# Attention and SwiGLU on one core: the q and k loads of five pairs spread over all partitions, heads paired h and h+4, dummy matmuls in early gaps

## The chip, the cores and the metric

The kernel runs on one core of one Trainium2 chip. The time is device microseconds of that core, from the start of the program to its end. Three runs of the kernel before took 261.69, 265.27 and 265.81 us; the median is 265.27. The profile below is of one further execution, which took 262.36 us.

## The reference

Two steps follow each other. The first is attention for 4 batches, 8 heads, 768 positions and head size 64. Heads 0, 2 and 6 are retrieval heads with the full causal mask; the other five are streaming heads, which keep the first 4 positions (sinks) and a window of 64.

```python
scores = scale * np.matmul(q, k.transpose(0, 1, 3, 2))
causal = rel >= 0
stream_keep = causal & (is_sink | in_win)      # is_sink: pos < 4; in_win: 0 <= rel < 64
mask = np.where(retrieval_head, causal, stream_keep)
a = softmax(np.where(mask, scores, -1e9))
x = np.matmul(a, v)                            # heads side by side: 3072 tokens x 512
```

The second is a SwiGLU block on the 3072 tokens, with weights 512 x 1536, 512 x 1536 and 1536 x 512.

```python
g = x @ w_gate
silu = g * (1.0 / (1.0 + np.exp(-g)))
return (silu * (x @ w_val) @ w_out).astype(np.float32)
```

q, k, v and the weights come in float32; the kernel's matmuls work in float16.

## The kernel before

**Pairs and tiles.** Positions are worked on in tiles of 128. Two tiles of one batch form a pair: 12 pairs, in the order of `QP` (L150), which alternates batches 0 and 1 first. A pair needs three loads of 512 KB: q, k and V (`load`, L332). A load lands in one of 14 `raw` buffers in float32, and is cast to float16 by ACT, DVE or POOL (`cast` for q and k, `castv` for V).

**Turning q and k.** Scores need head dimension on the partitions. For the first five pairs (`n < XPE`, XPE = 5) PE does it: `transposes` makes eight 128x128 transposes of the cast buffer into PSUM, and `evac` copies each half of the pair from there into `qT` or `kT`, with a strided read. For the later pairs a DMA transpose does it (`dmat`). After either, two heads lie one above the other: one on partitions 0 to 63, the other on 64 to 127. Which two is said by `PAIRS`, now (0,2), (4,6), (1,3), (5,7) (L165).

**How the first five pairs are loaded.** There are two DMAs for each of q and k, one for each four heads. Each writes 64 partitions: a partition gets, for each of four heads, four neighbouring rows of 64 floats, so runs of 1 KB. V is always loaded in one DMA over 128 partitions in runs of 512 B; gate and value weights over 128 partitions in runs of 1 KB; output weights over 128 partitions in runs of 2 KB.

**Scores to x.** `plan` (L473) lists for each tile units of up to eight 128x128 score blocks. `scores` multiplies them into two PSUM banks; in the first four tiles (LEAD = 4) masks are added there by PE through `marks`. `exps` takes the exponential on ACT. Later tiles multiply by 0/1 masks m0, m1, m2 on DVE or POOL (`mask`, L553); `mask_fills` makes these masks on DVE early on. `sinks_k` and `sinks_v` copy the sink positions into the blocks of the streaming heads. `values` multiplies with V, which has a column of ones for the sums; `norm` divides; x is turned again by PE (first eight tiles) or DMA.

**The feed-forward block** takes groups of four tiles: `gate` (L725, for gate and value products), tanh on ACT, two products on DVE (L735, L742), `outproj` (L760), a copy out and a store.

**What sets the order.** It is written out. `ORDER` is a list of task numbers, two characters each; tasks are emitted in that order, so it fixes the order on every engine's queue, the DMA issues on SP's included. `WAYS` picks the engine of a task that has a choice, `SLOTS` the buffer or PSUM bank. An engine works strictly through its own order, and a task waits for its inputs and for the earlier users of its buffer. SP issues k0, q0, q1, k1, q2, V0, k2, V1 first, then weights of the first group mixed with V2, k3, q3, k4, V3, q4 (the number is the pair).

**Warming products.** The task `warm` is the first on PE: ten matmuls of the identity with itself (L314), whose result nobody reads.

Of the kernel before, what the change touches and what calls it, by code (L numbers as in the profile page):

```python
# [16 lines left out]
    "070004011K1L061I1J09031T1Q1R1S1o1p1w1x1U1V1y1W1X1f1g0A1q1r1z021d1k1e0C2K202223212B2C2Q2R2S292G2A"  # L17
    "081O1N1P1M1h1Y1Z1a1i1j0D2L2T0B1t1s1u2425261b1c1v2D2E2F2U2W2V2X2Z2a27282c2d1m1n2I2J052Y2b2h2l2m2n"
    "2r2s2o2w0h138r8s8t9192938w8x8y0n14948z90958p8u0E2O2P2N2M8m8n8o8q8v1l0g0z8c8d8e8h8i8j0y8S8T8U8X8Y"
    "0m118k8f8g8Z8l108a8V8W8b2p2q0i169697989B9C9D2e2f2i2g0G31393A3B0l1F9a9b9c9f9g2t2u2v2x0F30360o179E"  # L20
    "9F9h37383F3G3I3J0r1G9d9i9e9j3C3P3D3E3K3L0k1C9V9Q9W9X9R9S3b3c3T3H999A3U3V0J3j3r3s3t0H3234333M3N35"
    "3O3W3X3Y3Z3a0q1D9Y9Z0I3i3o9T9U3p3q3u3x3v3w3y3z0j199G9H9I9L9M9N2j3R3S2k2y2z3Q3d3e3f0p1A9O9J9P0Q55"
    "54523g3h45484E4F0x4041A9AAABAdAeAfA7ATAUACADAV0PAgAh494A2H530u0t15AOAP0w1E18AQARASAnAoAp0MA4A551"
    "580s9KA6A812AJAKAL0v1B0O1HAMAN0K3m3k3l3n0L4MAEAWAXAH0RAFAGAI0S5U590V669k9l9m9n4SAYAZAaAi4T0N4Q4R"
    "4P4N4U4V50579oAsAtAu56AvAw0Z5b4B4J4C4D42434644470cAjAk9p9q9r9s9t4G4H4K4I4LAlAmAxAyAz4Z4a4b4W4X4Y"
    "4e4f9u9v9w9x4j4p4q4u4v4c4d5T5a5Z0U4r9zA0A1A2A34m4s4O4g4t4h4n4i4k4l4oAqArAbAc0T5X5W5H5I5J5A5B5C5K"
    "B2B0B10d7o6E9y4w4x6o6l7E6n4y4z5L7G5M656C6BB3B4B5B7B8B9BABBBCBDBEBFBGBt5Q5d5j5k5e5f5g5h5iBvBwBx5Y"
    "C3BqBrBsBu0Y0bCACBCCBgBhBiBMBN0W686967ByBzBOC0C15N5O5R5P5cCDCEC2C40a7C6DBPBQBlBmBnC5C6C7BWBX5V5D"
    "5E5F5G5SBjBkBYBUBZBa6k6s6r5o5u5r5v5s5wBoBp0XC8C95l5m5p5n5q626L6M5x7I5yBbBcBdBeBf5t5z60636164BRBS"
    "BTBV7D7L7KCFCGCH7HBHBIBJBKBLCICJ6I6J6K6F6G6H6S6N6OCoCpCqCKCLCMCN0fDXDYDZCjCkClD8D9DaDbDADBDC6j6p"  # L30
    "6q7374756t6u70797JDNDODPDG0e7p7wCyCz6P71726Q6R6U6TCrCsD0D1D26Y6Z6a6d6eDQDRDDDEDFDH6v6V6W6X7SD6D3"
    "D4D5D7CeCfCgCPCQCRCSCT6m767T777A787B6w6x7r6yChCiCtCuCv6b6c7u7v7P7Q7R7MCOCwCxCmCnDSDTDU6A6f6g6h6i"
    "7N7OCUCVCWCXCZCaCYCbCc7F7U7V7WDVDW7X7g7h7a7b7c7t7d7e7f6zE4ELEJEMEOE1E2EGENEPEfEgE3E5EiEhEHEIEKEk"
    "ElEmDIDJDKEBECDLDMEDB6EpEqEjErCdDcDdDeDfDh7Y7i7j7m7kEnEo7l84857y7z81828B8380DiDjDkDmDnDo86877x8E"
    "8H8I8FDrDsDtDu7q7Z7n8K8M888N898A8C8D8LEd8GEVEWEXEQEREEEFESEYEZEsEt7s8O8J8P8QDwDxDyDzE6E7E8E9EAEa"
    "EbEcEeETEU8RFJFKFsFEFLFtFWG2FuFTFUFFDvDpFiDqDlE0FVFXFjFkFHFlFnFoFqDgFmFpFrEuFGFIFMFNGAG3G4G7G8G9"
    "GBFYFZFaFxFyFbFcFzG0G1FRG5G6FOFPFvFwFQFSFgEvEwExEyEzF0FdFeFfFhGCF1F2F4F5F6F9FAFBFCF3FDF7F8GDGEGF"
    "GGGHGIGJGKGLGMGNGOGRGPGSGTGQGWGUGVGXGY"
# [3 lines left out]
    "000000000000220020220220011011000000000000000100220222011000000000000001201000000000002001222221"  # L42
    "001001000001000000001010000000000000002201000010010000000000020000000000000020202222000000000000"
    "000001100010000000000012012200000000000001001000020220220000000100000000100001001000002200222020"
    "000000000000000001000000000000000200200000000100000010000000101110210000001000000001200000000000"
    "021020200200000010000000000020000001000000000000000000000000000000000000000000000000000000000000"
    "000000000000000000000000000000000000000001000010000000000000000000000000000000000000000000000000"
    "000000000000000100001100000000010000000000000000000000000000000000000000000000000000000000000001"
    "100001000000001000000000000000000000000000000000000000000000000000000000000000010000110001000010"
    "000000000000000000000000000000000000000000000000000000000000000000000000000000010000000000000000"  # L50
    "0000000000000000000000000000000000000000000000001000100001000001010"
)
SLOTS = (
    "010523746A20796974080CAB6C17BD2493518B8DA51C93B8452163D10106040102241611232063220254440040006220"
    "616201436425612211161624043604454120646214300622320400616445611440622523226261404460004562163226"
    "112612440602263216203446045226106560612261304342246160122543246012162406140236445612242206143605"
    "0023111440102212311231000040220111550227010245020E1113A11049001182013501026303102104125F1004B212"
    "4I3021G3111D1000H0001M4112C1020K2010L2120J1121N0110024000104502081005A11046310472024E51010001511"
    "1243311152025211109021000124000M1011K1000G1120J4105I5120H0121F4001D002280020C4000L2122B100112025"
    "1149401142003241221502260123N5022541137510030103A111100004E521122000114M3002D2003C5012G4000H2110"  # L60
    "L1015J2011K5121B2101I301080101F310012011"
# [57 lines left out]
def kernel(  # L119
# [45 lines left out]
    PAIRS = [(0, 2), (4, 6), (1, 3), (5, 7)]  # L165
# [115 lines left out]
    def mask_fills(x):  # L281
        def run():
            for dst, src in FILLS[x]:
# [3 lines left out]
    FILLS = [[(m0[:, 0:3], BAND0), (m0[:, 3:4], DIAG), (m0[:, 4:6], BAND0), (m0[:, 6:8], DIAG),  # L287
              (m2[:, 2:5], DIAG), (m2[:, 1:2], OWN), (m1[:, 0:2], OWN)],
             [(m2[:, 0:1], FAR), (m1[:, 2:4], FAR)]]

    kT = [const.tile([128, NT, 2, 2, 128], FH, name=f"kT{n}") for n in range(2)]
    QB = 3
# [14 lines left out]
    warm_ps = []  # L307

    def warm(n=10):

        if not warm_ps:
            warm_ps.append(buf("o", [128, 512], FP, "warm"))
        for _ in range(n):
            nc.tensor.matmul(warm_ps[0], ident, ident.unsqueeze(1).to_broadcast([128, 4, 128]),  # L314
                             start=True, stop=True)
# [3 lines left out]
    T_fill1 = P.add("fill1", ["POOL"], fill1)  # L319
    T_warm = P.add("warm", ["PE"], warm, takes=["o"])  # L320
# [11 lines left out]
    def load(kind, n):  # L332
        r = buf("raw", [128, 1024], FP, "raw")
        landed[kind, n] = r
        if kind in "qkx":
            b, pi = QP[n]
            sl = slice(pi * 256, (pi + 1) * 256)
            if kind != "x" and n < XPE:
                for s_ in range(2):
                    nc.sync.dma_start(  # L340
                        out=r[64 * s_:64 * s_ + 64, :].rearrange("p (f x) -> p f x", f=4),
                        in_={"q": q, "k": k}[kind][b, 4 * s_:4 * s_ + 4, sl, :].rearrange(
                            "f (p j) d -> p f (j d)", j=4))
                return
            nc.sync.dma_start(
                out=r.rearrange("p (h x) -> p h x", h=H),
                in_={"q": q, "k": k, "x": v}[kind][b, :, sl, :].rearrange(
                    "h (p j) d -> p h (j d)", j=2))
        elif kind == "o":
            nc.sync.dma_start(  # L350
                out=r.rearrange("p (a n) -> p a n", a=2), in_=wod[:, 2 * n:2 * n + 2, :])
        else:
            nc.sync.dma_start(
                out=r.rearrange("p (a n) -> p a n", a=4),
                in_=(wgd if kind == "g" else wvd)[:, :, n * 256:(n + 1) * 256])
# [46 lines left out]
    def cast(n, kd, x):  # L402
# [4 lines left out]
        if n < XPE:  # L407
# [6 lines left out]
        ks = slice(0, 2) if x is None else slice(x, x + 1)  # L414
        recast(T_c[n, kd, x],
               hqs[n, kd][:, ks].rearrange("p k a (s d) -> p k s a d", s=2),
               landed[kd, n].rearrange("p (k s r j d) -> p k s (r j) d", r=2, s=2, j=2, d=64)[:, ks])
# [24 lines left out]
    def transposes(n, kd):  # L442

        tr = trs[n, kd] = buf("gv", [128, 8, 128], FH, "tr")
        for x in range(8):
            r, j = x // 4, x % 4
            to = x if kd == "q" else 4 * r + 2 * (j % 2) + j // 2
            nc.tensor.transpose(tr[:, to], hqs[n, kd][:, r, j], ident)

    def evac(n, kd, m):  # L450

        dst = turned(n, kd)[:, m].rearrange("c k r x -> c (k r x)")
        if kd == "q":
            copy(T_ev[n, kd][m],
                 dst.rearrange("c (k r p j) -> c k r p j", k=2, r=2, j=4),
                 trs[n, kd].rearrange("c (r j) (k m p) -> c m k r p j", r=2, k=2, m=2)[:, m])
            return
        copy(T_ev[n, kd][m],
             dst.rearrange("c (k l p i) -> c k l p i", k=2, l=4, i=2),
             trs[n, kd].rearrange("c (l i) (k m p) -> c m k l p i", i=2, k=2, m=2)[:, m])  # L460

    def sinks_k(b, m):
# [3 lines left out]
        for cs, k, r in ((slice(0, 128), slice(0, 2), 1), (slice(0, 64), slice(1, 2), 0)):  # L466
# [8 lines left out]
    def plan(t):  # L475

        b, i = TILES[t]
        if i == 0:
# [4 lines left out]
              ([(0, 0, 0, 0), (0, 1, 5, i), (1, 0, 1, -1), (1, 1, 4, i),  # L483
                (1, 0, 2, i), (1, 1, 6, 0), (0, 0, 3, i), (0, 1, 7, 0)], 8, m2)]
        kts = list(range(1, i))
        for ks in (kts[:2], kts[2:]):
            unit = []
            for x, kt in enumerate(ks):
                unit += [(0, 0, 4 - len(ks) + x, kt), (0, 1, 4 + 2 * x, kt),
                         (1, 1, 5 + 2 * x, kt)]  # L490
            if unit:
                us.append((unit, 4 + 2 * len(ks), None))
        return us

    def marks(t, u):
# [3 lines left out]
        if TILES[t][1] == 0:  # L499
            return [(0, BAND0, 3), (3, DIAG, 1), (4, BAND0, 2), (6, DIAG, 2)]  # L500
        if u == 0:
            return [(0, OWN, 2), (2, FAR, 2), (4, OWN, 2), (6, FAR, 2)]
        return [(1, FAR, 1), (2, OWN, 1), (3, DIAG, 1), (4, DIAG, 2)]

    def block(t, p, kt):
# [3 lines left out]
        return kT[b % 2][:, kt, p % 2, p // 2]  # L509
# [8 lines left out]
    def scores(t, u, unit):  # L518
# [4 lines left out]
        for p, s_, c, kt in unit[0]:  # L523
            rows = slice(s_ * 64, s_ * 64 + 64)
            terms.append((c, 1, block(t, p, kt)[rows],
                          qT[t // 2 % QB][rows, half, p % 2, p // 2].unsqueeze(1)))
# [20 lines left out]
    def mask(task, t, u, m):  # L547
        at = 1 if m is m2 else 0
# [286 lines left out]
    for number in P.order():  # L835
# [3 lines left out]
        else:  # L839
            warm(number - P.FILL)  # L840
# [35 lines left out]
```

## Time and profile before

| what | us |
|---|---|
| median of three runs | 265.27 |
| lowest and highest | 261.69, 265.81 |
| the profiled execution's own time | 262.36 |
| its span, first to last instruction | 260.5 |
| PE busy | 243.2 (93%) |
| VectorE (DVE) busy | 165.9 (64%) |
| ScalarE (ACT) busy | 139.2 (53%) |
| GpSimd (POOL) busy | 84.1 (32%) |
| bytes read from HBM | 28.31 MB |
| granted TensorE clock, mean | 0.993 |

A row of digits in the page cuts the span into 40 slices of 6.5 us; a digit is the busy share in tenths, 9 for 90% and more. PE is TensorE's matmuls, PEld its weight loads, SP the engine that issues most DMAs. PEclk is the clock that TensorE was granted. In the chain of waits a line says when a piece began, how long it was, and what it was; the chain goes back from the last instruction through whatever released each step. In a timeline the bracket at the end is the idle time before an instruction, with what ended it.

The PE clock row needs care in the first 18 us. It shows full clock there, but the ten warming products start 0.43 us apart, and later products of the same 512 columns 0.22 us apart.

### The profile page before, as it was taken

The page shows a single profiled execution, that of the slowest core. Times are in us where ns is not written, and L with a number is a line of the kernel's source. Part 1 is how long each engine was busy: PE and PEld are TensorE (multiplying, and loading weights), DVE is VectorE, ACT ScalarE, POOL GpSimd, SP SyncE. Part 2 cuts the span into 40 slices and gives each one's busy share as a digit, 9 for nine tenths or more (in the row PEclk, how much of TensorE's full clock was granted, in tenths as well). Part 3 has the DMA queues.
Part 4 walks back from the last instruction along what each step waited for, and adds up shares of the span by engine and source line. Part 5 has one row for each costly group of instructions (what it writes and reads, how often), then busy time and mean ns, then how long its engine had stood idle before and what let it go on. Part 6 is the DMA issues. An engine that isn't in the chain of part 4 may idle for free.

```text
span 260.5 us, 5165 instructions
## 1 busy us (share of the span) xinstructions
PE 243.2 (93%) x1998; PEld 127.9 (49%) x1998; DVE 165.9 (64%) x294; ACT 139.2 (53%) x219; POOL 84.1 (32%) x114
## 2 busy tenths in 40 slices
PE   6597987969999899989999999999999999999995
PEld 2365764446444445534464454555454554444443
DVE  2338897768497974609989678646773477883211
ACT  1568874738677476647585476644526713421120
POOL 7057945675432354183051018240014200000000
PEclk9999999979999999999999999999999999999999
DMA  6999999999699989999258841344010021101133
GB/s 152 230 236 325 285 219 264 226 273 332 155 327 276 236 168 220 300 254 255 45 77 177 193 102 20 83 116 128 1 23 20 20 64 52 69 3 40 40 126 115
DMA packets 68007, 40.69 MB, mean 156 GB/s; under 512 B 25360, under 2 KB 63504, under 8 KB 67984
## 3 DMA queue, kind: packets, MB, share of 16 engines
q1 hardware_dynamic: 66832, 38.35, 63.5%
q10 hardware_dynamic: 1152, 2.03, 2.1%
q8 instruction: 15, 0.25, 0.4%
q14 instruction: 8, 0.07, 0.1%
HBM read 28.31 MB, written 6.29 MB: 133 GB/s over the span
## 4 chain that ended last, share of the span: by engine, by line
PE 73%; DMA 13%; DVE 6%; SPq 3%; issue 2%; POOL 1%; ACT 1%; DVEq 0%; ACTq 0%
PE banks L725 40%; PE banks L760 22%; DMA raw<-in_v_dram 8%; PE banks L533 5%; PE banks L563 5%; SPq L340 3%; DMA kT<-hq 2%; DMA raw<-in_q_dram 2%; DVE e L553 2%; DVE sil L735 1%; DVE h L742 1%; POOL vt L206 1%; DVE xb L571 1%; PE banks L587 0%; POOL hq L206 0%
## 5 line engine op out<-in xcount | busy, mean ns | idle before, releaser
L545 ACT ACTIVATE e<-banks 128x1024 f16<-128x1024 f32 (+2 forms) x68 | 58.4, 908 | 31.0 <-PE banks L533 22.4
L725 PE MATMUL banks<-xt,wv_sb 128*128 128x512 f16 (+1 forms) x304 | 71.2, 371 | 2.8 <-POOL wv_sb L206 1.5
L725 PE MATMUL banks<-xt,wg_sb 128*128 128x512 f16 (+1 forms) x304 | 69.3, 368 | 1.6 <-POOL wg_sb L206 1.5
L731 ACT ACTIVATE sig<-banks 128x512 f32<-128x512 f32 (+1 forms) x76 | 43.1, 575 | 43.7 <-PE banks L725 38.5
L760 PE MATMUL banks<-wo_sb,h 128*128 128x512 f16 (+2 forms) x300 | 64.8, 371 | 0.0
L735 DVE SCALAR_TENSOR_TENSOR sil<-sig,banks 128x512 f32<-128x512 f32 (+1 forms) x76 | 49.3, 657 | 19.3 <-ACT sig L731 17.4
L742 DVE SCALAR_TENSOR_TENSOR h<-sil,banks 128x512 f16<-128x512 f32 (+1 forms) x76 | 49.0, 656 | 7.8 <-PE banks L725 5.0
L725 PEld LDWEIGHTS <-wg_sb 128*128 128x128 f16 x304 | 28.8, 97 | 33.1 <-POOL wg_sb L206 1.8
L725 PEld LDWEIGHTS <-wv_sb 128*128 128x128 f16 x304 | 28.3, 98 | 32.5 <-issue 2.8
L760 PEld LDWEIGHTS <-h 128*128 128x128 f16 x300 | 28.3, 98 | 32.4 <-issue 0.3
L553 POOL TENSOR_TENSOR e<-e,m 128x1024 f16<-128x1024 f16 (+1 forms) x12 | 22.6, 1883 | 32.4 <-ACT e L545 26.1
L553 DVE TENSOR_TENSOR e<-e,m 128x640 f16<-128x640 f16 (+1 forms) x26 | 20.3, 786 | 16.8 <-ACT e L545 16.6
L206 DVE COPY o_sb<-banks 128x512 f32<-128x512 f32 (+1 forms) x13 | 8.6, 660 | 25.0 <-PE banks L760 23.0
L206 POOL CAST vt<-raw 64x512 f16<-64x512 f32 x27 | 18.2, 675 | 17.7 <-DMA raw<-in_v_dram 14.3
L206 POOL CAST hq<-raw 128x1024 f16<-128x1024 f32 (+1 forms) x16 | 15.8, 989 | 24.7 <-DMA raw<-in_q_dram 11.9
L563 PE MATMUL banks<-vt,e 128*128 128x65 f16 x472 | 18.6, 195 | 4.0 <-POOL vt L206 3.1
L533 PE MATMUL banks<-qT,kT 64*128 64x128 f16 x472 | 21.0, 223 | 0.6 <-ACT e L545 0.4
L563 PEld LDWEIGHTS <-e 128*128 128x128 f16 x472 | 17.4, 98 | 8.4 <-issue 4.6
L204 ACT COPY o_sb<-banks 128x512 f32<-128x512 f32 (+1 forms) x12 | 6.9, 577 | 26.9 <-PE banks L760 23.1
L533 PEld LDWEIGHTS <-kT 64*128 64x128 f16 x472 | 15.1, 96 | 11.4 <-issue 10.0
L571 DVE TENSOR_TENSOR xb<-banks,rc 128x512 f16<-128x512 f32 x24 | 16.6, 691 | 0.8
L206 POOL COPY vt<-vt 2x330 f16<-2x330 f16 x12 | 5.8, 481 | 27.4 <-PE banks L563 27.1
(41 smaller groups left out, 117.2 us busy)
## 6 DMA issues: line engine op xcount, KB each, us to landing
raw<-in_v_dram SPq DMA_DIRECT2D x12, 512.0 KB, 7.5
out_dram<-o_sb SPq DMA_DIRECT2D x16, 256.0 KB, 2.3
raw<-in_k_dram SPq DMA_DIRECT2D x7, 512.0 KB, 5.9
raw<-in_q_dram SPq DMA_DIRECT2D x7, 512.0 KB, 5.8
raw<-in_moe_w_gate_dram SPq DMA_DIRECT2D x6, 512.0 KB, 9.8
raw<-in_moe_w_val_dram SPq DMA_DIRECT2D x6, 512.0 KB, 11.5
raw<-in_moe_w_out_dram SPq DMA_DIRECT2D x6, 512.0 KB, 8.0
raw<-in_k_dram SPq DMA_DIRECT2D x10, 256.0 KB, 9.0
```

What stands on the lines that cost most here:

```text
L206: ENG[task.way].tensor_copy(out=dst, in_=src)
L340: nc.sync.dma_start(out=r[64 * s_:64 * s_ + 64, :].rearrange("p (f x) -> p f x", f=4), in_={"q": q, "k": k}[kind][b, 4 * s_:4 * s_ + 4, sl ...
L533: nc.tensor.matmul(sc[:, c:c + n, :], weights, moving, start=first, stop=last)
L545: nc.scalar.activation(out=to, in_=src, func=AF.Exp, scale=scale)
L553: ENG[task().way].tensor_tensor(out=ev, in0=ev, in1=mm, op=ALU.mult)
L563: nc.tensor.matmul(avs[t][:, odd, n * 66:n * 66 + 65], ee, vv, start=(m == 0), stop=(m == len(bl) - 1))
L571: nc.vector.tensor_tensor(out=xb.rearrange("p n o d -> p o n d"), in0=av[:, :, :, 0:64], in1=rc.to_broadcast([128, 2, 4, 64]), op=ALU.mult)
L725: nc.tensor.matmul(ps, wsb[:, kk, j * 128:(j + 1) * 128], xt[:, kk, c[0]:c[1]], start=(kk == 0), stop=(kk == 3))
L731: nc.scalar.activation(out=sg[g, j, c], in_=gs[g, j, c], func=AF.Tanh, scale=0.5)
L735: nc.vector.scalar_tensor_tensor(out=sl[g, j, c], in0=sg.pop((g, j, c)), scalar=1.0, op0=ALU.add, in1=gs.pop((g, j, c)), op1=ALU.mult)
L742: nc.vector.scalar_tensor_tensor(out=hs[g, j][:, c[0]:c[1]], in0=sl.pop((g, j, c)), scalar=0.5, op0=ALU.mult, in1=vs.pop((g, j, c)), op1=A ...
L760: nc.tensor.matmul(o_open[g, tt, x], hs[g, j][:, tt * 128:(tt + 1) * 128], wo_sb[:, j, lo:hi], start=(j == 0), stop=(j == NJ - 1))
```

## The change

**Loads of the first five pairs.** Each of the two DMAs now writes all 128 partitions: for four heads, a partition gets eight neighbouring rows of one head, a run of 2 KB, in one half of the buffer's columns. Bytes, number of DMAs and their order on SP stay.

**Heads paired h and h+4.** With that layout a cast puts heads h and h+4 one above the other, so `PAIRS` becomes (2,6), (0,4), (1,5), (3,7). Blocks in `plan`, columns of the masks, `marks`, `sinks_k`, `block` and the cast of the later pairs follow from it. The number and sizes of score blocks, exponentials and masks stay. `evac` reads the transposes with other strides, in the same two copies of 512 columns.

**Warming products.** `warm` takes a count and a PSUM bank. PE's order gets 7 ahead of the transposes of k0, 3 ahead of those of q0 and 5 ahead of those of q1.

**The order.** ORDER, WAYS and SLOTS are written anew. Decoded, PE's order is otherwise the same but for a dozen neighbours that change places, and SP's is the same up to its 45th issue. The tasks that change engines: the cast of k1's first half POOL to ACT; the sink copy of tile 1 ACT to POOL, ahead of V's first casts; two V casts (pairs 9 and 11) ACT to POOL; one mask DVE to POOL; two output copies ACT to DVE; two stores SP to ACT.

```diff
 ORDER = (
...
 WAYS = (
...
 SLOTS = (
...
-    PAIRS = [(0, 2), (4, 6), (1, 3), (5, 7)]
+    PAIRS = [(2, 6), (0, 4), (1, 5), (3, 7)]
...
-    FILLS = [[(m0[:, 0:3], BAND0), (m0[:, 3:4], DIAG), (m0[:, 4:6], BAND0), (m0[:, 6:8], DIAG),
-              (m2[:, 2:5], DIAG), (m2[:, 1:2], OWN), (m1[:, 0:2], OWN)],
-             [(m2[:, 0:1], FAR), (m1[:, 2:4], FAR)]]
+    FILLS = [[(m0[:, 0:2], BAND0), (m0[:, 2:4], DIAG), (m0[:, 4:7], BAND0), (m0[:, 7:8], DIAG),
+              (m2[:, 0:3], DIAG), (m2[:, 3:4], OWN), (m1[:, 0:2], OWN)],
+             [(m2[:, 4:5], FAR), (m1[:, 2:4], FAR)]]
...
-    def warm(n=10):
-
-        if not warm_ps:
-            warm_ps.append(buf("o", [128, 512], FP, "warm"))
-        for _ in range(n):
-            nc.tensor.matmul(warm_ps[0], ident, ident.unsqueeze(1).to_broadcast([128, 4, 128]),
+    def warm(n=10, at=None):
+        if at is None:
+            to = buf("o", [128, 512], FP, "warm")
+        else:
+            to = banks[:, at * 512:at * 512 + 512]
+        for x in range(n):
+            nc.tensor.matmul(to, ident, ident.unsqueeze(1).to_broadcast([128, 4, 128]),
                              start=True, stop=True)
...
             if kind != "x" and n < XPE:
                 for s_ in range(2):
                     nc.sync.dma_start(
-                        out=r[64 * s_:64 * s_ + 64, :].rearrange("p (f x) -> p f x", f=4),
+                        out=r[:, 512 * s_:512 * s_ + 512],
                         in_={"q": q, "k": k}[kind][b, 4 * s_:4 * s_ + 4, sl, :].rearrange(
-                            "f (p j) d -> p f (j d)", j=4))
+                            "f (p j) d -> p f (j d)", j=8))
...
     def transposes(n, kd):
 
         tr = trs[n, kd] = buf("gv", [128, 8, 128], FH, "tr")
-        for x in range(8):
-            r, j = x // 4, x % 4
-            to = x if kd == "q" else 4 * r + 2 * (j % 2) + j // 2
-            nc.tensor.transpose(tr[:, to], hqs[n, kd][:, r, j], ident)
+        for j in range(8):
+            nc.tensor.transpose(tr[:, j], hqs[n, kd][:, j // 4, j % 4], ident)
...
         if kd == "q":
-            copy(T_ev[n, kd][m],
-                 dst.rearrange("c (k r p j) -> c k r p j", k=2, r=2, j=4),
-                 trs[n, kd].rearrange("c (r j) (k m p) -> c m k r p j", r=2, k=2, m=2)[:, m])
+            copy(T_ev[n, kd][m], dst.rearrange("c (f n j) -> c f n j", f=4, j=8),
+                 trs[n, kd].rearrange("c j (m n f) -> c m f n j", m=2, f=4)[:, m])
             return
...
-        return kT[b % 2][:, kt, p % 2, p // 2]
+        return kT[b % 2][:, kt, PAIRS[p][0] // 2, PAIRS[p][0] % 2]
...
         else:
-            warm(number - P.FILL)
+            warm((number - P.FILL) % 16, (number - P.FILL) // 16)
```

## The prediction

> **What bounds the kernel now.** First the page's rows of the span in 40 slices (6.5 us each), then the table by stage: time, then busy us and instructions of PE, PEld, DVE, ACT and POOL, then granted clock, DMA share, GB/s.
>
> ```profile
> PE   6597987969999899989999999999999999999995
> PEclk9999999979999999999999999999999999999999
> DMA  6999999999699989999258841344010021101133
> 0.00:18.00 18.00, 12.88 (x86) 6.94 (x88) 5.90 (x14) 7.24 (x12) 7.99 (x26) 1.00 0.97 203
> 18.00:39.00 21.00, 18.20 (x252) 14.10 (x252) 17.11 (x42) 17.40 (x32) 14.58 (x21) 1.00 1.13 273
> 39.00:57.00 18.00, 13.60 (x150) 7.96 (x151) 12.84 (x23) 9.20 (x14) 11.03 (x12) 0.93 1.13 248
> 57.00:258.00 201.00, 198.56 (x1516) 98.88 (x1514) 130.06 (x216) 105.34 (x164) 50.53 (x57) 1.00 0.55 132
> ```
>
> From 57 us to the end PE is busy 198.56 of 201 us: that part is a fixed sum of matmuls, and the DMA engines idle half of it. Before 57 us PE is busy only 44.7 of 57 us while the DMA engines are full in every slice. So the first 57 us are bound by loads, and what they gain is handed to the end nearly whole.
>
> Next, the same table for PE alone, over stretches chosen by what is in flight (last column GB/s):
>
> ```profile
> 3.00:13.50 10.50, 6.74 (x35) 1.00 1.12 236
> 21.00:30.00 9.00, 8.02 (x136) 1.00 1.12 330
> 30.00:39.00 9.00, 7.63 (x77) 1.00 1.13 216
> 42.00:54.00 12.00, 8.37 (x84) 1.00 1.15 217
> 57.00:66.00 9.00, 9.00 (x110) 0.95 1.05 333
> 54.00:55.50 1.50, 1.29 (x27) 0.66 1.11 252
> 55.50:57.00 1.50, 1.50 (x17) 0.50 1.13 320
> 57.00:58.50 1.50, 1.50 (x13) 0.70 1.14 317
> ```
>
> In 3 to 13.5 us only q and k of pairs 0 to 2 move: 236 GB/s. In 21 to 30 us gate and value weights and one V load: 330, at the same DMA share. Where k3 and q3, then k4 and q4 are mixed in: 216 and 217. Last, the chain of waits (start, us) and PE's timeline:
>
> ```profile
> 12.45 9.37 DMA raw<-in_v_dram
> 39.64 12.19 DMA raw<-in_v_dram
> 54.21 1.34 PE banks L563 x25
> 1.36 4.45 PE L314 MATMUL banks<-ident 128*128 128x512 f16 x10 [1.36 <-POOL ident L226]
> 39.56 1.90 PE L725 MATMUL banks<-xt,wg_sb 128*128 128x512 f16 x8 [1.47 <-POOL wg_sb L206]
> 45.67 1.90 PE L725 MATMUL banks<-xt,wv_sb 128*128 128x512 f16 x8 [1.01 <-POOL wv_sb L206]
> 54.21 1.34 PE L563 MATMUL banks<-vt,e 128*128 128x65 f16 x25 [2.32 <-POOL vt L206]
> ```
>
> The chain goes through V of pair 1 (landing at 21.8) and V of pair 3 (51.8, 12 us after its issue: it queues behind other loads). PE waits there for casts that wait for DMA.
>
> **Loads.** The ten q and k loads keep their places in SP's order. Only their shape changes: 2 DMAs of 64 partitions x 4 runs of 1 KB become 2 of 128 partitions x one run of 2 KB. The Trainium skill's "DMA: Bandwidth & Descriptors", in its opening table, puts the line rate at runs of 512 B and more; by it 1 KB runs have nothing to gain and the time stays at 262 to 265. The rows speak otherwise: weight loads in 1 KB runs over 128 partitions and V in 512 B runs make the 330, so run length is not what makes 236. What is left is the half of the partitions; "SBUF — State Buffer", "Door 1: The DMA port swizzle", says that partitions 0..63 reach only 8 of 16 ports, about 218 GB/s. I follow the rows and take 330 GB/s for the new loads (bounds: 236, nothing gained, and the 376 of the best 1.5 us, where the weights for the output run in 2 KB runs).
>
> Worked out: by 54 us the stage rates sum to 13.0 MB. Ten loads of 0.524 MB are 5.24 MB of it; the other 7.76 MB at 330 take 23.5 us, the first bytes come at about 2.6 us, so q and k had 27.9 us (188 GB/s). At 330 they need 15.9: DMA is 12.0 us ahead by then. Of that, the first five (2.62 MB) go from 11.1 to 7.9 us, so V of pair 0 lands 3.2 us sooner. The last five go from 16.8 to 7.9, 1.8 each: V of pair 1 (one more in front) 5.0 sooner, V of pair 3 (four more) some 10.
>
> **Start, to the first value products (20.64 us).** They wait for V of pair 0, then four POOL casts (2.60 us). 3.2 to 4.4 us is to be had. Three things could hold it.
> - The 15 warming products stand ahead of the first three transposes. At the spacing of the old ten (0.43 us) they cost 6.4 us, at 0.22 (12 products in 2.75 us later on) 3.2. The gaps that they fill are 1.80, 0.65 and 1.32 = 3.77 us now and will shrink with the loads, so this cover goes. Ten plus seven in a row keep PE busy from 1.4 us on; I expect full speed from about 7 us, so 3 of them cold, 12 warm, 3.9 us. Then the third transposes start near 10.7 (now 11.73). The work from there to 20.4 that ran at half speed until 16 (128x128 transposes at 1.03 us for eight, 0.62 later) saves 2 to 3 us. PE is ready at about 17, as V is. Bounds: +2.6 us if all stay cold against today's gaps, -3.6 (half of 7.2 us of cold rows).
> - Cast of k1's first half goes from POOL to ACT, ahead of the first exponential: 0.61 us into a hole of 1.62. Behind it stand all exponentials, but k1 lands before the scores are done. Nothing.
> - The sink copy of tile 1 goes from ACT to POOL, ahead of V's first casts: it waits for tile 1's scores, and the four casts and val1 wait behind it. 0.4 us of copies, 0 to 0.6 of waiting; ACT loses a wait of 1.01. I take 0.4.
>
> Sum: 3.5 us sooner (bounds 1.0 and 4.6).
>
> **18 to 39 us** move along: DVE has 17.1 of 21 us of work, so nothing more is gained.
>
> **39 to 57 us.** Here PE waits 1.47, 0.50 and 1.01 us for weight casts and 2.32 for V of pair 3, all behind loads that now come 5 to 10 us sooner. The floors are DVE 12.84 and PE 13.60 less its cold share. That share: 0.34 x 1.29 + 0.5 x 1.5 = 1.2 us, and 0.45 after 57. "TensorE: Matmul & The Clock Gate", "What's actually happening", has the clock fall after an idle window of some 3.4 us; by it a gap of 2.3 us costs nothing, and the gain would be the waits alone. The row shows 0.66 and 0.50 right after that gap, so I count 1.6 us for its going. POOL is next in line: after the mask product (1.41) it casts k4 and V (1.5 and 2.28) in order, 5 us after the exponential, while PE has some 6 us of other work. So the stretch takes about 14 us instead of 18, and 0.4 is saved after it: 4.4 (bounds 2.5, where POOL's order keeps half of the waits, and 5.6, at DVE's floor).
>
> **Everything else.** Evacuations, masks, scores, mask fills and sink copies keep their counts and sizes (two evacuations of 512 columns per transposed half, masks of 1024 and 640): only strides and columns differ. An evacuation costs 0.59 to 0.69 us now with a strided read of PSUM too; at 10% either way 20 of them are 1 us on DVE and ACT, mostly covered. I take 0. Later moves: one V cast of pair 9 to POOL (its POOL hole of 104 to 109 covers 0.6), one mask to POOL (+0.6), two output copies ACT to DVE, two stores from SP to ACT's queue (0.4 of issue each): all where PE has work queued; 0, without that cover 0.7 us each. Stage four has 2.4 us of PE waits: 1 us either way.
>
> **Sum.** 3.5 + 4.4 = 7.9 us off the profiled execution's 262.36 (span 260.5 and 1.9 around it): 254.5. The median shown, 265.27, lies 2.9 above that run, the fastest 261.69. I put half of that on top: **256.0**.
>
> **Rivals.**
> 1. *Taken back by order* (0.15): the warming products stay cold and POOL's order keeps half of the waits: gains 1.0 and 2.5, 258.9, with the same half 260.3. For it: POOL's fixed order, and DVE at 17 of 21 us. Against: POOL has 7 of 18 us free.
> 2. *The loads are no faster* (0.08): 236 comes from something else that q and k have, say head stride. The dummies then fill today's gaps and run 0.1 to 2.6 us over, the clock gives that back: 264 to 266. Against: V has the same head stride and moved in the 330.
> 3. *Slower* (0.06): neighbouring partitions now come from four heads, 196 KB apart, and that access lowers the rate. Break-even is 188 GB/s; at 150 the ten loads take 34.9 us instead of 27.9, all of it on the chain to V of pair 3: 272. Against: V's eight-head loads. It decides if the first stretch shows under 190.
>
> **Numbers.** The forecast has 0.68 (252 to 260), 0.03 lies below. The range takes in the best bounds (10.2 off: 252.2) and rival 1 with the whole offset (258.9 + 2.9 = 261.8). 2% is 5.3 us, about what a measurement of this kernel can tell from no change: under 260.0 is faster. Faster 0.72 (forecast nearly whole, some of rival 1), same 0.20, slower 0.08.
>
> **What would show it.** 300 GB/s or more in 3 to 10 us; V of pair 0 cast from about 15 us; transposes of eight at 0.62 us before 12 us; no PE wait over 1 us for V of pair 3, no slice of the clock under 0.9; PE full from about 49 us; the same 198 to 199 us of PE after. Wrong if the first stretch stays near 236, if the warming products end well after the first casts, or if a wait of over 2 us appears after 60 us.

## The result and the profile after

The changed kernel takes 251.31 us (median of four runs, 250.07 to 252.32) against 263.48 us for the kernel before (four runs, 261.57 to 265.81). The ratio is 0.9556, with a 95% interval of 0.9464 to 0.9648. The prediction had the direction, but it was 256.0, and the measured median lies 0.7 us below the low end of its range, 252. Single executions that were over 1.5% slower than the fastest of their kernel count in the medians of this document, but not in its ratios. The profiled execution took 250.07 us, the shortest of the four, with a span of 248.3.

Two of the page's rows, as before, now in slices of 6.2 us, and the same table by stage (time, busy us and instructions of PE, PEld, DVE, ACT and POOL, granted clock, DMA share, GB/s):

```profile
PE   7999899999999999999999999999999999999995
PEclk9999999999999999999999999999999999999999
0.00:18.00 18.00, 16.47 (x161) 9.37 (x161) 7.57 (x19) 10.96 (x15) 11.21 (x32) 1.00 0.90 285
18.00:39.00 21.00, 19.68 (x247) 14.68 (x248) 19.08 (x45) 16.53 (x32) 15.67 (x21) 1.00 1.10 348
39.00:57.00 18.00, 17.96 (x210) 10.30 (x208) 15.19 (x29) 15.22 (x26) 14.42 (x17) 1.00 0.88 276
57.00:245.00 188.00, 187.38 (x1398) 92.62 (x1397) 123.48 (x204) 94.89 (x144) 45.33 (x49) 1.00 0.51 122
```

Between 39 and 57 us PE now works 17.96 of 18 us (13.60 before), and the clock no longer drops. PE is full from about 27 us on, 30 us earlier than before. DVE went to 19.08 of 21 us and to 15.19 of 18. The table for PE alone over stretches (last column GB/s):

```profile
3.00:10.00 7.00, 7.00 (x36) 1.00 0.95 319
20.00:30.00 10.00, 8.94 (x110) 1.00 1.09 357
30.00:39.00 9.00, 8.91 (x106) 1.00 1.10 347
39.00:45.00 6.00, 5.96 (x66) 1.00 1.11 341
```

Loads move at 319 GB/s and more from the start; the stretches of 216 and 217 are gone. Adding up the rates, the 13.0 MB that took 54 us before are in after 40.6 us (12.4 MB by 39 us, the rest at 341 GB/s). PE's timeline (start, us, what, and in brackets any wait) at the places that were shown of before:

```profile
1.36 6.71 PE L314 MATMUL banks<-ident 128*128 128x512 f16 x17 [1.36 <-POOL ident L227]
7.91 0.61 PE L446 MATMUL banks<-ident,hq 128*128 128x128 f16 x8
16.78 1.17 PE L562 MATMUL banks<-vt,e 128*128 128x65 f16 x24
33.42 0.61 PE L446 MATMUL banks<-ident,hq 128*128 128x128 f16 x8
33.87 1.89 PE L724 MATMUL banks<-xt,wg_sb 128*128 128x512 f16 x8
38.42 2.10 PE L724 MATMUL banks<-xt,wv_sb 128*128 128x512 f16 x8
44.59 0.92 PE L562 MATMUL banks<-vt,e 128*128 128x65 f16 x25
47.03 0.62 PE L446 MATMUL banks<-ident,hq 128*128 128x128 f16 x8
```

Two rows of the kernel before, for the same transposes as those at 33.42 and 47.03:

```profile
37.48 0.61 PE L448 MATMUL banks<-ident,hq 128*128 128x128 f16 x8
58.02 0.61 PE L448 MATMUL banks<-ident,hq 128*128 128x128 f16 x8
```

None of the rows of the changed kernel after the first has a bracket: the waits of 1.47, 1.01 and 2.32 us are gone. The 25 value products that need V of pair 3 take 0.92 us instead of 1.34; the clock was 0.66 there and is 1.00 now. ("Cold" below means a clock of about half, "warm" the full one.) Followed by the start of the same work, the gain builds up like this:

| the same work | before | after | gain so far | predicted so far |
|---|---|---|---|---|
| first value products | 20.64 | 16.78 | 3.9 | 3.5 |
| transposes just ahead of the wait of 1.47 us | 37.48 | 33.42 | 4.1 | 3.5 |
| gate products that waited 1.47 us | 39.56 | 33.87 | 5.7 | |
| value products after V of pair 3 | 54.21 | 44.59 | 9.6 | |
| transposes of the fifth q | 58.02 | 47.03 | 11.0 | 7.9 |
| end of the last matmul | 257.48 | 245.22 | 12.3 | 7.9 |

### The profile page after: what moved, and what is told of

Read it like the earlier page. It is cut to its first block, busy times and chain, and to the rows that moved or that the text cites. A ratio compares the mean times of both kernels' runs of the same rounds, so it can differ in the third digit from the quotient of the medians.

```text
span 248.3 us, 5185 instructions
## 1 busy us (share of the span) xinstructions
PE 241.7 (97%) x2013; PEld 127.0 (51%) x2013; DVE 165.6 (67%) x295; ACT 137.7 (55%) x214; POOL 86.6 (35%) x118
## 4 chain that ended last, share of the span: by engine, by line
PE 85%; DVE 7%; ACT 2%; issue 2%; DMA 2%; POOL 1%; DVEq 0%; POOLq 0%; ACTq 0%
PE banks L724 46%; PE banks L759 22%; PE banks L532 6%; PE banks L562 5%; PE banks L314 3%; DVE e L552 2%; DMA out_dram<-o_sb 2%; DVE sil L734 1%; PE banks L446 1%; ACT e L544 1%; DVE xb L570 1%; POOL vt L207 1%; DVE o_sb L207 1%; DVE h L741 1%; PE banks L586 0%
## 5 line engine op out<-in xcount | busy, mean ns | idle before, releaser
L552 POOL TENSOR_TENSOR e<-e,m 128x1024 f16<-128x1024 f16 (+1 forms) x13 | 24.0, 1854 | 38.8 <-ACT e L544 31.2
L207 DVE COPY o_sb<-banks 128x512 f32<-128x512 f32 (+1 forms) x15 | 9.9, 663 | 27.5 <-PE banks L759 23.6
L207 POOL CAST vt<-raw 64x512 f16<-64x512 f32 x29 | 19.6, 676 | 16.5 <-DMA raw<-in_v_dram 11.5
L552 DVE TENSOR_TENSOR e<-e,m 128x640 f16<-128x640 f16 (+1 forms) x25 | 19.0, 773 | 8.6 <-ACT e L544 8.4
L207 POOL CAST hq<-raw 128x1024 f16<-128x1024 f32 (+1 forms) x15 | 15.2, 1016 | 17.9 <-DMA raw<-in_q_dram 7.1
L532 PE MATMUL banks<-qT,kT 64*128 64x128 f16 x472 | 20.1, 217 | 0.7 <-ACT e L544 0.4
L532 PEld LDWEIGHTS <-kT 64*128 64x128 f16 x472 | 14.6, 94 | 10.9 <-issue 8.8
L205 ACT COPY o_sb<-banks 128x512 f32<-128x512 f32 (+1 forms) x10 | 5.8, 576 | 23.2 <-PE banks L759 22.6
## 6 DMA issues: line engine op xcount, KB each, us to landing
out_dram<-o_sb SPq DMA_DIRECT2D x14, 256.0 KB, 2.4
raw<-in_k_dram SPq DMA_DIRECT2D x10, 256.0 KB, 6.4
```

Of the source, the lines that this page charges most:

```text
L207: ENG[task.way].tensor_copy(out=dst, in_=src)
L532: nc.tensor.matmul(sc[:, c:c + n, :], weights, moving, start=first, stop=last)
L552: ENG[task().way].tensor_tensor(out=ev, in0=ev, in1=mm, op=ALU.mult)
```

## The experiments

**Partitions or run length.** The change spreads a DMA over all partitions and doubles its runs at once. Two kernels do one each. Both read other rows of q and k, the same in both kernels, to get that shape with the same bytes and the same number of DMAs (`r0` is 0 or 256).

```diff
-                        out=r[:, 512 * s_:512 * s_ + 512],
-                        in_={"q": q, "k": k}[kind][b, 4 * s_:4 * s_ + 4, sl, :].rearrange(
+                        out=r[64 * z:64 * z + 64, :].rearrange("p (f x) -> p f x", f=2),
+                        in_={"q": q, "k": k}[kind][b, 2 * z:2 * z + 2, r0:r0 + 512, :].rearrange(
                             "f (p j) d -> p f (j d)", j=8))
```

> The changed kernel, but each DMA of q and k of the first five pairs writes 64 partitions with two runs of 2 KB each (the same 256 KB, the same number of DMAs and of runs). To get that shape the rows are taken from other places of q and k, so the scores are of other rows and the output is not the reference's; all instructions after the loads are the same. Theory A, the partitions make the rate: 216 to 240 GB/s from 3 to 13 us as before, and 258 to 264 us. Theory B, the run length makes it: over 300 GB/s there, and 250 to 253 us.

```diff
+                        out=r[:, 512 * z:512 * z + 512].rearrange("p (f x) -> p f x", f=2),
+                        in_={"q": q, "k": k}[kind][b, 2 * z:2 * z + 2, r0:r0 + 512, :].rearrange(
+                            "f (p j) d -> p f (j d)", j=4))
```

> The counterpart: each of these DMAs writes all 128 partitions, with two runs of 1 KB each (256 KB; twice as many runs; rows again taken from other places, so the output is not the reference's). Theory A, the partitions: over 300 GB/s from 3 to 10 us, and 250 to 254 us. Theory B, the run length: 216 to 240 GB/s, and 258 to 264 us.

Measured: 64 partitions with 2 KB runs 261.94 us, ratio to before 1.0009 (0.9978 to 1.0041); 128 partitions with 1 KB runs 251.43 us, ratio 0.9615 (0.957 to 0.966). The stretch in which q and k move alone, first of the half, then of the full width:

```profile
3.00:13.50 10.50, 10.49 (x82) 1.00 1.06 243
```

```profile
3.00:13.50 10.50, 10.50 (x84) 1.00 1.03 321
```

Theory A holds at both ends. With 2 KB runs on half of the partitions nothing is gained, and with 1 KB runs on all of them the whole gain is there, within the intervals. In the changed kernel itself this stretch shows 329 GB/s, so of the step from 236 to 329, doubling the runs makes 7 to 8 GB/s (236 to 243 on half of the partitions, 321 to 329 on all). The first of the two kernels also has the new pairing, order and warming products: without the wider loads these bring nothing.

**Loads without the plan, plan without the loads.** The first is the changed kernel with ORDER, WAYS and SLOTS of before, the second the kernel before with those of the changed one and its `warm`.

> New loads and new pairing of heads, but with the order, engines and buffers of before and without the fifteen warming products. If the loads carry the gain: 251 to 254 us, PE free of waits over 1 us between 35 and 50 us. If the new order and the warming products carry a good part of it: 256 to 260.

> Loads and pairing of before, with the new order, engines and buffers and the fifteen warming products. If the loads carry the gain: 261 to 265 us, as before, and the fifteen products fill waits for the loads. If the order or the products carry a good part: 255 to 260. If the products run past the loads: up to 267.

Loads alone: 253.11 us, ratio 0.9699 (0.9636 to 0.9762). Plan alone: 262.63 us, ratio 1.0 (0.9957 to 1.0043). So the loads carry some 8 to 9 us by themselves. Order and warming products together add 2 to 4 us (1.8 by the medians, 3.1 to 3.7 by the ratios), but only on top of the loads. In plan alone the first value products do come 1.9 us sooner than before (18.75 against 20.64), because V of pair 0 is cast from 16.79 instead of 18.67; why it lands sooner with the same loads was not tried. By the first gate products this lead is gone (27.86 against 27.42). PE's timeline there, and its clock (busy us, instructions, granted clock, DMA share, GB/s):

```profile
18.75 0.19 PE L562 MATMUL banks<-vt,e 128*128 128x65 f16 x1 [1.35 <-POOL vt L206]
18.00:20.00 2.00, 0.78 (x13) 0.83 1.17 286
20.00:22.00 2.00, 1.69 (x24) 0.50 1.10 345
46.00:48.00 2.00, 1.18 (x7) 0.66 0.99 258
48.00:50.00 2.00, 2.00 (x6) 0.50 0.96 186
```

PE has been warmed up, but then waits for V of pair 0 and falls to half speed at 20 us, and again at 48 us, after waits for weight casts. In this kernel the warming is lost in the waits that follow it; the kernel with 64 partitions and 2 KB runs shows the same (a wait of 1.41 us for V, then a clock of 0.59 and 0.50 from 20 to 24 us).

**How many warming products.** The count at the three places is changed, all else stays. None first:

```diff
-            warm((number - P.FILL) % 16, (number - P.FILL) // 16)
+            n = {7: 0, 3: 0, 5: 0}[(number - P.FILL) % 16]
+            if n:
+                warm(n, (number - P.FILL) // 16)
```

> The changed kernel without its fifteen warming products; all else stays. If they only keep the clock up at the start and the start waits for V of pair 0 anyway: the first transposes begin at 6.7 us instead of 7.9 but run cold, the first value products stay within 0.5 us of 16.8, and 251 to 252 us. If the clock matters on the path: first value products at 17.5 or later, clock under 1 in the first 18 us, and 252 to 254.

> The changed kernel with 14, 6 and 10 warming products in place of 7, 3 and 5. If PE has time to spare before the first value products: 250 to 252 us. If the fifteen are on the path already, as the chain of waits of the changed kernel says, fifteen more at 0.22 us each put the start back by 3.3 us: 254 to 255.

None: 253.99 us, ratio 0.965 (0.9579 to 0.9722). PE starts sooner and arrives later:

```profile
6.64 0.92 PE L446 MATMUL banks<-ident,hq 128*128 128x128 f16 x8 [1.07 <-ACT hq L205]
13.15 1.04 PE L446 MATMUL banks<-ident,hq 128*128 128x128 f16 x8
18.40 1.07 PE L562 MATMUL banks<-vt,e 128*128 128x65 f16 x24
```

Its transposes still run at 1.04 us for eight at 13 us (0.61 in the changed kernel from 7.9 on), and the first value products come at 18.40, 1.6 us later, without any wait for V. So in this execution the cold array is what sets the start. But loads alone has none of the fifteen products either, and starts almost as early as the changed kernel:

```profile
17.11 1.12 PE L562 MATMUL banks<-vt,e 128*128 128x65 f16 x24
```

Its PE waits by much the same 1.07, 0.85 and 0.52 us ahead of the first transposes (1.07, 0.74 and 0.51 without products), and yet its clock is back at 0.96 in 12 to 14 us, where the kernel without products shows 0.50, and 0.64 in 14 to 16. What brings the clock up sooner in one of them was not tried. So the products are worth 0.3 to 1.6 us at the start, by which of the two they are compared with. Nor does the new order show a gain by itself: with the new loads but without the products the ratio is 0.965 with it and 0.9699 without it, and the intervals overlap.

Double: 258.31 us, ratio 0.9833 (0.975 to 0.9916). The start is back by 3.3 us as expected (20.06), but the end by 6 to 7, past the expected 254 to 255. Two waits for DVE near 40 us (0.74 and 0.42) and these new ones make the rest:

```profile
85.93 0.68 PE L532 MATMUL banks<-qT,kT 64*128 64x128 f16 x18 [0.94 <-DMA kT<-hq]
144.88 0.85 PE L532 MATMUL banks<-qT,kT 64*128 64x128 f16 x24 [1.45 <-DMA qT<-hq]
```

Both are for DMA transposes of later pairs. The kernel without warming products has one too, of 2.17 us at 84.45. The written order fits one timing; why a late start meets these transposes worse was not tried.

**Which loads.** The new loads for pairs 0 to 2 alone, then for pairs 3 and 4 alone; the others take the DMA of the first experiment (64 partitions, 2 KB runs). The second kernel has `n < 3` in this place.

```diff
                 for s_ in range(2):
+                    if n >= 3:
+                        z = s_
+                        nc.sync.dma_start(
+                            out=r[64 * z:64 * z + 64, :].rearrange("p (f x) -> p f x", f=2),
...
+                        continue
```

> The changed kernel with the new loads for pairs 0 to 2 alone; pairs 3 and 4 are loaded by DMAs of 64 partitions with two runs of 2 KB (rows from other places, so the output is not the reference's). If the gain adds up by stage, as the prediction has it: the start keeps its 3.9 us, the waits for weight casts and for V of pair 3 between 39 and 57 us come back in part (two to three loads of 1.8 us each before V of pair 3): 254 to 257 us. If the early loads alone free the later ones: 251 to 253.

> The reverse: pairs 3 and 4 in the new form, pairs 0 to 2 in DMAs of 64 partitions (rows from other places, so the output is not the reference's). If the gain adds up by stage: the start is as late as before (first value products at 18.5 us or later), the waits of 39 to 57 us go: 255 to 259 us. If the end depends on the last of these loads alone and PE catches up: 251 to 253.

Early alone: 258.15 us, ratio 0.9817 (0.9712 to 0.9922), past the expected 254 to 257. Late alone: 257.64 us, ratio 0.9718 (0.9593 to 0.9843), from two executions of 253.98 and 256.97; expected were 255 to 259. The two gains of 1.8% and 2.8% make 4.6% together, about the 4.2 to 4.4% of the whole change. That fits gains that add up, as those of a chain of separate waits would; with intervals of more than a percent to either side it does not prove it. In the early kernel the start is as in the changed one. The wait for V of pair 3 is as in the kernel before, and the waits for weight casts are about two thirds of those before (0.83, 0.34 and 0.70 us against 1.47, 0.50 and 1.01):

```profile
16.20 0.19 PE L570 MATMUL banks<-vt,e 128*128 128x65 f16 x1 [0.23 <-POOL vt L207]
34.63 1.90 PE L732 MATMUL banks<-xt,wg_sb 128*128 128x512 f16 x8 [0.83 <-POOL wg_sb L207]
49.02 0.91 PE L570 MATMUL banks<-vt,e 128*128 128x65 f16 x25 [2.44 <-POOL vt L207]
```

At the transposes of the fifth q it has gained 6.0 us (52.04 against 58.02). After that PE waits 3.4 us in all, against 1.8 in the kernel before, and 1.8 us of the gain are lost by the last matmul; that is why it misses its range.

**A better count?** Doubling showed that the products stand on the path. Two smaller counts were run beside the changed kernel itself: 4, 1, 2 and 7, 1, 1.

> The changed kernel as it is, as the yardstick for the next two on the same chip: 250 to 252.5 us.

> The changed kernel with 4, 1 and 2 warming products in place of 7, 3 and 5. Doubling them put the first value products back by 3.3 us and the end by some 7, so they are on the path. If eight fewer at 0.22 to 0.43 us bring the start forward while the clock still comes up before 9 us: first value products at 16.0 to 16.5, and 249 to 251 us. If fewer of them leave the clock down, as without any (first value products 18.4): 252 to 254.

> The changed kernel with the 7 in front kept, which bring the clock up, and 1 and 1 in place of 3 and 5. If those six stand on the path and are not needed once the clock is up: the third transposes some 0.6 us sooner, 249.5 to 251 us. If V of pair 0 sets the start (its casts end at 17.0): no difference from the changed kernel within 0.5 us.

The changed kernel again: 251.15 us, 0.958 (0.9532 to 0.9628). With 4, 1, 2: 250.84, 0.9565 (0.9525 to 0.9604). With 7, 1, 1: 251.84, 0.9609 (0.9558 to 0.9659). There is no difference between the three. With 4, 1, 2 the third transposes come 0.7 us sooner (9.88 against 10.55), and then the value products wait for V:

```profile
9.88 0.62 PE L446 MATMUL banks<-ident,hq 128*128 128x128 f16 x8 [0.41 <-POOL hq L207]
16.64 0.86 PE L562 MATMUL banks<-vt,e 128*128 128x65 f16 x23 [0.29 <-POOL vt L207]
```

The first of them comes at 16.14, 0.6 us sooner than in the changed kernel, the other 23 at 16.64 after this wait. So with fewer products V of pair 0 is the next bound of the start, and little is to be had there.

## Why the prediction was right and wrong

**What bounds the kernel: right.** The loads did bound the first 57 us (though the first slice of the DMA row, a 6, was not full), and what they gained went to the end whole: 11.0 us by the fifth q's transposes, 12.3 at the last matmul.

**The loads: right, and a little low.** The partitions make the rate and not the run length; the first two experiments show it. The rule on run length that the prediction cites would put all of these loads at the same rate; measured were 243 GB/s with 2 KB runs on half of the partitions and 321 with 1 KB runs on all, so by itself it does not tell them apart. The ports that it cites show in no row; the 236 and 243 GB/s of DMAs to alternating halves lie above the 218 cited for one half. Taken were 330 GB/s, measured 319 to 357; DMA is 13.4 us ahead at the 13.0 MB mark (12.0 predicted).

**The start: right.** 3.9 us for 3.5. Four of the seven first warming products ran cold (2.3 us for seven, from 0.43 and 0.22 each), where three were assumed; the third transposes began at 10.53 (10.7 predicted). From there to the first value products it took 6.3 us instead of 8.9, 2.7 saved where 2 to 3 were forecast. The sink copy that was moved to POOL made it wait 0.75 us for the scores, ahead of V's casts (0 to 0.6 predicted); those still ended at 17.0, as predicted.

**18 to 39 us: right for its own work, wrong at its edge.** Between the first value products and the transposes at 37.48 only 0.2 us more was gained. Of PE's waits there, 0.48 us for V went, and 0.36 for ACT and 0.46 for DVE stayed (0.35 and 0.62 after). But 0.9 of the 1.47 us that PE then waits for a weight cast lies before 39 us, in the stage that was put at nothing.

**39 to 57 us: this step failed, in its size.** The prediction lists PE's waits of 1.47, 0.50, 1.01 and 2.32 us and 1.6 us of cold time, 6.9 us in all, and then gives 4.4. From the transposes just ahead of the first of these waits to those of the fifth q the gain grew from 4.1 to 11.0 us: all 6.9 came, more than the best bound of 5.6. Two terms were mis-sized.
- The stretch was held at about 14 of its 18 us by the orders of DVE and POOL. It was not: the work between 39.56 and 58.02 us, 18.5 us before, took 13.2 after (33.87 to 47.03), with no wait of PE over 0.4 us. In it PE was busy for 13.0 us and DVE for 12.1, so PE set the pace. POOL's mask, k4 and V took 4.8 us, as foreseen, but began at 39.64 instead of 47.93, and the casts ended 0.2 us before PE was ready for V: near, but no wait.
- The 1.47 us wait was listed in this step, but the step was worked out from the 18 us after 39, which hold only 0.6 of it.

Of the shortfall of 4.4 us (12.3 less 7.9), 2.5 come from this step, 0.4 from the start, 0.2 from 18 to 39 us and 1.3 from the time after 57 us. The low end of the range rested on 10.2 us of best bounds, and this step alone went past its bound by 1.3.

**After 57 us: a little past its margin of 1 us, and partly luck.** PE waited 1.8 us there before (0.84, 0.79, 0.15) and 0.4 in the profile after. The repeated kernel has 1.5 us of such waits and the same median within 0.2 us. The new loads with the old order have 2.9 in all, with 0.93 and 0.78 at the same places as before.

**The other moves: right at nothing** for the plan alone, with a ratio of 1.0; on top of the new loads no run takes them apart from the warming products beyond doubt.

**The rivals.** "Taken back by order" fell: the products came up to speed, and POOL's order kept no wait. "The loads are no faster" and "slower" fell with 319 GB/s in the first stretch. That half of the offset between profile and median came true (1.24 us after, 1.45 taken) is luck: the repeated kernel's profiled execution lay 0.98 us above its median, not below.

## What to carry to other kernels

Where an engine is bound by data, write down its own waits and its cold time in the stretch: here their sum, 6.9 us, came back whole, and a busy share of 71% on another engine (DVE, 12.84 of 18 us) was no floor. Follow the same work through both kernels, since a wait that straddles the edge of two stages is easily counted in neither. Look at how many partitions a DMA writes before looking at its run length. In these runs dummy matmuls paid at most where real matmuls followed without a wait for data.

## What the runs showed of the hardware

Pairs of DMAs to the two halves of the partitions, issued one after the other, moved 243 GB/s with 2 KB runs; the same bytes over all partitions moved 321 with 1 KB runs. Full-width loads queued among such half-width ones did not raise the rate: 216 and 217 GB/s in the kernel before against 236 for the half-width ones alone, 229 and 225 against 240 in plan alone.

The clock of the array fell without any long gap: in plan alone waits of 1.35 and 0.47 us, with PE busy for 0.78 of 2 us, were followed by 0.50. The length of one wait did not decide it: after 2.32 us in the kernel before the clock was 0.66 and 0.50, after 2.44 us in the kernel with the early loads alone it stayed at 1.00. And the clock row showed 1.00 in the first 8 us of the changed kernel, while its first ten products started 0.43 us apart, twice the spacing at full speed.
